# Layer one's sum holds h+1: an ELU from one Exp and one two-operand pass, and seven of eight steps of the second layer in split precision

## The chip, the core and the metric

One core of one Trainium2 chip. The metric is the device time of one launch in microseconds (us), median of three runs. Engines: TensorE (PE) multiplies matrices; VectorE (DVE), ScalarE (ACT) and GpSimd (POOL) work elementwise; SyncE (SP) issues the transfers. Matmuls write PSUM, everything else lies in SBUF.

## The reference

Agent attention and a two-layer network on its output. There are two batches of 12480 tokens of 128 channels, 49 agents, and a hidden width of 2048. Nothing but fp32 goes in and comes out, except for the weights, which are fp64.

```python
a2k = softmax(scale * agents @ k.T)          # per batch, 49 x 12480
agent_v = a2k @ v                            # 49 x 128
q2a = softmax(scale * q @ agents.T)          # 12480 x 49
x = (q2a @ agent_v).reshape(24960, 128)
h = x @ w_in                                 # 24960 x 2048
g = np.where(h > 0, h, np.exp(np.minimum(h, 0)) - 1)
out = g @ w_out                              # 24960 x 128
```

## The kernel before

**Layers.** `agent_v @ w_in` is folded into one matrix A of 49 rows and 2048 columns per batch, so the first layer is `h = q2a @ A`. The tokens come in 26 groups of 960 (13 per batch); a group has two halves of 480 columns. A half is worked through in eight steps (`NP`), each with 256 rows of the hidden width as two tiles of 128. That makes S = 416 steps. In a step:

- `p1` (matmul at L413) makes `h` of both tiles in two PSUM banks. Probabilities `p` and matrix A are both split into a high part in fp32r (fp32 cut to fewer bits) and a low part, the remainder. Products are high x high, high x low and low x high; the two tiles lie on rows 0 to 48 and 64 to 112 of the operands, so their matmuls run in pairs side by side.
- `elu` makes g: ACT computes `e = Relu(-h)` (L419) and `e = Exp(-e)` (L422) in place, DVE computes `g = max(e - 1, h)` (L424), reading `h` from PSUM.
- `split`, in the steps whose number modulo 8 is in `SPLITS`, makes `hi = fp32r(g)` on DVE (L431) and, in two passes on POOL, `lo0` and `lo1`, each `g - hi` of one tile (by the helper `rest`, L204). In the last step of all, those two run on DVE.
- `p2` (L453), four steps later (`LAG = 4`; three at the very start), adds the second layer of a step into two PSUM banks. A plain step multiplies g and `w_f` in fp32: four matmuls, which the profile shows as eight records. A split step has twelve in fp32r: hi x w_lo, hi x w_hi, lo x w_hi. Rows 0 to 63 and 64 to 127 go to different banks, again as pairs side by side.
- After the last of eight steps, the two banks are added: DVE copies one (`ob`, L465), ACT the other (`oa`, L468, called `rest_of_sum` and placed between Relu and Exp of the step), POOL adds them (L469) and SP stores.

**Order.** The order of each engine's queue is written out by hand: the main loop at the end (from L719) issues per step `p1`, `p2` of four steps before, the work listed in `mid`, `elu`, `split`, then the work listed in `pre` by `at(s, ...)`. Engines run their queues in order. `h` has three slots in PSUM, shared with the attention's work; tile `e` has 2 buffers, `g` 5, `hi` 3, `lo0` and `lo1` 3 each.

**Attention among the steps.** The scores and maxima of the groups of q, and for the second batch those of k and the sum with v, are done in visits (`plan`, `visit`): in some steps, one slot of PSUM takes the scores of two groups (L291, L160), and DVE and ACT turn them into probabilities over the next steps (maxima L296, L303, Exp L307, sums L311, `pp` L325, transposes L331, parts `px` and `py` L345 to L350). In the late half there is one visit with two q groups in every 32 steps.

**Prologue.** Before the loop the first batch's attention is done, and the fp64 weights are turned into fp32 by integer steps (`f64_steps`, whose ACT passes are L103 and L105), `w_out` also into `w_f`, or `w_hi` (ACT, L199) and `w_lo` (POOL, L204). At the end stand the sum with v (L219), its transposition (L238, L239) and A for the first batch (L257, `A_hi`, `A_lo`). At s = 2 there is one matmul (L731) whose result nobody reads.

```python
    SPLITS = ((1, 3, 4, 6, 7), (1, 4, 6, 7))

    def is_split(s):
        j, half, c = at_step(s)
        return c in SPLITS[half if j * NM + NP + LAG in covered else 0]
```

So a half has five or four split steps; in the late part of the kernel 19 of 32.

Of the kernel before, what the change touches and what calls it, by code (L numbers as in the profile page):

```python
# [24 lines left out]
def tile_agent_attention_moe(  # L25
# [14 lines left out]
    NA2 = ROWS[1] + NA  # L40
# [23 lines left out]
    wc_p = ctx.enter_context(tc.tile_pool(name="wc", bufs=2))  # L64
# [272 lines left out]
    def q_parts(j, part):  # L337
# [10 lines left out]
        a, b = [slice(r, r + NA) for r in ROWS]  # L348
# [15 lines left out]
    def wo_step(c):  # L364

        if c not in wo_gen:
            parts = []
            for i in range(2):
# [4 lines left out]
                else:  # L373
                    w_e[x] = wc_p.tile([128, 256], F32, tag="even", name="even")
# [41 lines left out]
    def elu(s, between=None):  # L416

        h, e = h_t.pop(s), x_p.tile([128, 2, T], F32, tag="e", name="e")
        nc.scalar.activation(out=e, in_=h, func=ACTF.Relu, scale=-1.0)  # L419
        if between:  # L420
            between()
        nc.scalar.activation(out=e, in_=e, func=ACTF.Exp, scale=-1.0)  # L422
        g = g_p.tile([128, 2, T], F32, tag="g", name="g", bufs=5)
        nc.vector.scalar_tensor_tensor(out=g, in0=e, scalar=-1.0, in1=h, op0=ALU.add, op1=ALU.max)  # L424
        g_t[s] = g

    def split(s):
        if not is_split(s):
            return
        hi_t[s] = g_p.tile([128, 2, T], F32R, tag="hi", name="hi", bufs=3)  # L430
        nc.vector.tensor_copy(out=hi_t[s], in_=g_t[s])  # L431
        lo_t[s] = []
        for i in range(2):
            lo_t[s].append(g_p.tile([128, T], F32R, tag=f"lo{i}", name=f"lo{i}", bufs=3))
            rest(nc.vector if s == S - 1 else nc.gpsimd, lo_t[s][i], g_t[s][:, i, :], hi_t[s][:, i, :])

    def p2(s):
# [16 lines left out]
        if last:  # L454
# [325 lines left out]
```

## Time and profile before

| | |
|---|---|
| median of three runs | 998.79 us (998.23 to 1000.27) |
| profiled execution, first to last instruction | 995.9 us |
| PE, DVE, ACT, POOL busy | 978.3, 849.7, 884.3, 687.0 us |
| mean granted clock of PE | 0.996 |

The profile is of one execution, for which the page gives the span from first to last instruction and no other time; the runs' times have 2.9 us around it at the median. Times inside are us from the start of the span; an engine's busy time is the union of its instructions. Matmuls overlap in the pipeline, so the mean duration of one is no price; the chain's pieces are.

### The profile page before, as it was taken

The page shows a single profiled execution, that of the slowest core. Times are in us where ns is not written, and L with a number is a line of the kernel's source. Part 1 is how long each engine was busy: PE and PEld are TensorE (multiplying, and loading weights), DVE is VectorE, ACT ScalarE, POOL GpSimd, SP SyncE. Part 2 cuts the span into 40 slices and gives each one's busy share as a digit, 9 for nine tenths or more (in the row PEclk, how much of TensorE's full clock was granted, in tenths as well). Part 3 has the DMA queues.
Part 4 walks back from the last instruction along what each step waited for, and adds up shares of the span by engine and source line. Part 5 has one row for each costly group of instructions (what it writes and reads, how often), then busy time and mean ns, then how long its engine had stood idle before and what let it go on. Part 6 is the DMA issues. An engine that isn't in the chain of part 4 may idle for free.

```text
span 995.9 us, 25483 instructions
## 1 busy us (share of the span) xinstructions
PE 978.3 (98%) x10380; PEld 734.3 (74%) x10380; DVE 849.7 (85%) x1028; ACT 884.3 (89%) x1017; POOL 687.0 (69%) x559
## 2 busy tenths in 40 slices
PE   7899999999999999999999999999999999999998
PEld 5767777777777777877777777777777777777775
DVE  7778888888888878888888898898888888988887
ACT  4588998988988889998998999989999989989996
POOL 3146666666666766766786886877868867867886
PEclk8999999999999999999999999999999999999999
DMA  9942222223232211101101101011020021001000
GB/s 349 385 148 89 80 72 81 78 74 96 68 85 66 66 41 46 38 31 65 36 23 55 37 26 62 26 56 41 18 76 27 21 66 37 26 12 37 27 20 21
DMA packets 25983, 67.30 MB, mean 68 GB/s; under 512 B 3083, under 2 KB 14963, under 8 KB 25867
## 3 DMA queue, kind: packets, MB, share of 16 engines
q1 hardware_dynamic: 25867, 65.69, 19.5%
q8 instruction: 81, 1.33, 0.6%
q14 instruction: 35, 0.29, 0.1%
HBM read 43.11 MB, written 12.78 MB: 56 GB/s over the span
## 4 chain that ended last, share of the span: by engine, by line
PE 93%; DVE 2%; ACT 2%; DMA 2%; issue 1%; POOL 0%; SPq 0%; DVEq 0%; ACTq 0%
PE o L453 59%; PE h L413 27%; PE h L291 2%; PE h L219 2%; PE h L160 1%; DMA v<-in_vx_dram 1%; PE h L331 1%; DVE g L424 1%; DMA k<-in_kT_dram 1%; ACT e L419 1%; ACT e L422 0%; PE o L160 0%; DVE m_all L168 0%; DVE ex L107 0%; ACT ex L103 0%
## 5 line engine op out<-in xcount | busy, mean ns | idle before, releaser
L204 POOL TENSOR_TENSOR lo<-g,hi 128x480 fp32r<-128x480 f32 x484 | 603.3, 1272 | 253.6 <-DVE hi L431 190.3
L424 DVE SCALAR_TENSOR_TENSOR g<-e,h 128x960 f32<-128x960 f32 x416 | 478.2, 1150 | 109.2 <-ACT e L422 91.7
L419 ACT ACTIVATE e<-h 128x960 f32<-128x960 f32 x416 | 402.5, 967 | 41.0 <-PE h L413 38.5
L422 ACT ACTIVATE e<-e 128x960 f32<-128x960 f32 x416 | 419.1, 1007 | 11.6
L453 PE MATMUL o<-g,w_f 64*128 64x480 f32 x1384 | 307.8, 562 | 0.2 <-DVE g L424 0.2
L413 PE MATMUL h<-py,ahi 49*128 49x480 f32 x832 | 292.4, 431 | 1.4 <-DVE g L424 0.7
L413 PE MATMUL h<-px,ahi 49*128 49x480 f32 x832 | 292.4, 431 | 0.1
L431 DVE CAST hi<-g 128x960 fp32r<-128x960 f32 x243 | 198.4, 816 | 10.8
L453 PEld LDWEIGHTS o<-g,w_f 64*128 64x128 f32 x1384 | 133.2, 185 | 83.1 <-issue 73.6
L413 PEld LDWEIGHTS h<-py,ahi 49*128 49x128 f32 x832 | 149.9, 186 | 39.3 <-issue 23.4
L413 PEld LDWEIGHTS h<-px,ahi 49*128 49x128 f32 x832 | 149.9, 186 | 26.3 <-issue 17.0
L453 PE MATMUL o<-hi,w_lo 64*128 64x480 f32 x972 | 159.4, 403 | 0.0
L413 PE MATMUL h<-px,alo 49*128 49x480 f32 x416 | 157.0, 377 | 0.0
L413 PE MATMUL h<-py,alo 49*128 49x480 f32 x416 | 157.0, 377 | 0.0
L453 PE MATMUL o<-lo,w_hi 64*128 64x480 f32 x972 | 146.9, 378 | 0.0
L453 PE MATMUL o<-hi,w_hi 64*128 64x480 f32 x972 | 146.0, 376 | 0.0
L453 PEld LDWEIGHTS o<-hi,w_lo 64*128 64x128 f32 x972 | 93.4, 186 | 26.0 <-issue 14.3
L453 PEld LDWEIGHTS o<-lo,w_hi 64*128 64x128 f32 x972 | 92.6, 184 | 13.6 <-POOL lo L204 0.3
L453 PEld LDWEIGHTS o<-hi,w_hi 64*128 64x128 f32 x972 | 92.5, 184 | 13.0
L413 PEld LDWEIGHTS h<-py,alo 49*128 49x128 f32 x416 | 76.6, 184 | 5.7
L413 PEld LDWEIGHTS h<-px,alo 49*128 49x128 f32 x416 | 76.6, 184 | 5.6 <-DVE alo L275 0.2
L469 POOL TENSOR_TENSOR ob<-ob,oa 128x480 f32<-128x480 f32 x51 | 70.0, 1372 | 12.2 <-ACT oa L468 12.2
(89 smaller groups left out, 517.7 us busy)
## 6 DMA issues: line engine op xcount, KB each, us to landing
k<-in_kT_dram SPq DMA_DIRECT2D x26, 480.0 KB
q<-in_qT_dram SPq DMA_DIRECT2D x26, 480.0 KB
out_dram<-ob SPq DMA_DIRECT2D x51, 240.0 KB
py<-px SPq DMA_DIRECT2D x104, 91.9 KB
v<-in_vx_dram SPq DMA_DIRECT2D x13, 516.0 KB
v<-in_vx_dram SPq DMA_DIRECT2D x13, 483.8 KB
raw<-in_w_in_dram SPq DMA_DIRECT2D x4, 512.0 KB
raw<-in_w_out_dram SPq DMA_DIRECT2D x4, 512.0 KB
```

The costliest lines, as they stand in the source:

```text
L160: nc.tensor.matmul(out=ps[u:u + w, j * NA:(j + 1) * NA], lhsT=src[:, x:x + w], rhs=ag_sb[:, b, :], start=True, stop=True)
L204: eng.tensor_tensor(out=out, in0=x, in1=hi.bitcast(F32), op=ALU.subtract)
L219: nc.tensor.matmul(out=ps[u:u + 64], lhsT=e[:, j * NA:j * NA + 64], rhs=v_t[b, r][:, j, :], start=(r == rs[0] and j < 2), stop=(r == rs[-1 ...
L291: nc.tensor.matmul(out=ps[u:u + w, t * NA:(t + 1) * NA], lhsT=src[:, x:x + w], rhs=ag_sb[:, j // NG, :], start=True, stop=True)
L331: nc.tensor.transpose(ps[:NA2, u, i * HP:(i + 1) * HP], pp[x, i, 0:NA2], ident[x, x])
L413: nc.tensor.matmul(out=h[:, u, 0:T], lhsT=a[x, :], rhs=p[u ^ half][x, :], start=i == 0, stop=i == 2)
L419: nc.scalar.activation(out=e, in_=h, func=ACTF.Relu, scale=-1.0)
L422: nc.scalar.activation(out=e, in_=e, func=ACTF.Exp, scale=-1.0)
L424: nc.vector.scalar_tensor_tensor(out=g, in0=e, scalar=-1.0, in1=h, op0=ALU.add, op1=ALU.max)
L431: nc.vector.tensor_copy(out=hi_t[s], in_=g_t[s])
L453: nc.tensor.matmul(out=o_t[u][:, 0:T], lhsT=w[x], rhs=v[x, :], start=first and i == 0, stop=last and i == len(jobs) - 1)
L469: nc.gpsimd.tensor_tensor(out=ob, in0=ob, in1=oa, op=ALU.add)
```

## The change

**Sum.** Both rows of probabilities get a 50th row of ones (`NK = NA + 1`; written once into `pp`), and A's high part gets a 50th row of ones, by a bias tile `unit` that is 1 in that row and 0 elsewhere (`A_hi`). So PSUM holds h+1. ELU+1 is then `max(min(exp(h), 1), h + 1)`: ACT's single pass is `Exp(x - 1)`, with a bias tile `mone`, and DVE's pass takes minimum and maximum in one. The Relu is gone.

**Constant.** As g is too large by 1, the output is too large by the column sums of `w_out`. `w_sums` has PE add these up from the weights' parts with matmuls of two columns, 22 in the prologue and 8 at s = 2 (in place of L731's), DVE negates them into `ncs`, and `oa` adds them as a bias.

**Split.** `PLAIN = (3,)`: one step in eight is plain. The cast to `hi` goes from DVE to ACT. Of the lo passes, `lo1` goes to DVE in steps 0, 2 and 7 of eight. `hi` has 4 buffers.

**Order.** `split` of a step is issued in the next step, after that one's `elu` and `rest_of_sum`. The pool of the conversions (`wc`) ends with the prologue.

```diff
-    SPLITS = ((1, 3, 4, 6, 7), (1, 4, 6, 7))
-    SPLIT = tuple(c for c in range(NP) if c in SPLITS[0] or c in SPLITS[1])
-    PLAIN = tuple(c for c in range(NP) if c not in SPLITS[0] or c not in SPLITS[1])
+    PLAIN = (3,)
+    SPLIT = tuple(c for c in range(NP) if c not in PLAIN)
+    LO_DVE = (0, 2, 7)
...
-            nc.scalar.activation(out=h, in_=A_ps(b, lo, hi), func=ACTF.Copy, scale=av["rz"][:, 0:1])
+            nc.scalar.activation(out=h, in_=A_ps(b, lo, hi), func=ACTF.Identity, scale=av["rz"][:, 0:1], bias=unit[:NA2, 0:1])
...
-                x = slice(r, r + NA)
+                x = slice(r, r + (NK if i == 0 else NA))
                 nc.tensor.matmul(out=h[:, u, 0:T], lhsT=a[x, :], rhs=p[u ^ half][x, :], start=i == 0, stop=i == 2)
...
-    def elu(s, between=None):
+    def elu(s):
 
         h, e = h_t.pop(s), x_p.tile([128, 2, T], F32, tag="e", name="e")
-        nc.scalar.activation(out=e, in_=h, func=ACTF.Relu, scale=-1.0)
-        if between:
-            between()
-        nc.scalar.activation(out=e, in_=e, func=ACTF.Exp, scale=-1.0)
+        nc.scalar.activation(out=e, in_=h, func=ACTF.Exp, bias=mone, scale=1.0)
         g = g_p.tile([128, 2, T], F32, tag="g", name="g", bufs=5)
-        nc.vector.scalar_tensor_tensor(out=g, in0=e, scalar=-1.0, in1=h, op0=ALU.add, op1=ALU.max)
+        nc.vector.scalar_tensor_tensor(out=g, in0=e, scalar=1.0, in1=h, op0=ALU.min, op1=ALU.max)
         g_t[s] = g
 
     def split(s):
-        if not is_split(s):
+        if not 0 <= s < S or not is_split(s):
             return
-        hi_t[s] = g_p.tile([128, 2, T], F32R, tag="hi", name="hi", bufs=3)
-        nc.vector.tensor_copy(out=hi_t[s], in_=g_t[s])
+        hi_t[s] = g_p.tile([128, 2, T], F32R, tag="hi", name="hi", bufs=4)
+        cast_hi(nc.scalar, hi_t[s], g_t[s])
         lo_t[s] = []
         for i in range(2):
+            eng = nc.vector if s == S - 1 or i and s % NP in LO_DVE else nc.gpsimd
             lo_t[s].append(g_p.tile([128, T], F32R, tag=f"lo{i}", name=f"lo{i}", bufs=3))
-            rest(nc.vector if s == S - 1 else nc.gpsimd, lo_t[s][i], g_t[s][:, i, :], hi_t[s][:, i, :])
+            rest(eng, lo_t[s][i], g_t[s][:, i, :], hi_t[s][:, i, :])
...
-                nc.scalar.activation(out=oa, in_=pa[:, 0:T], func=ACTF.Copy)
+                nc.scalar.activation(out=oa, in_=pa[:, 0:T], func=ACTF.Identity, bias=ncs[:, 0:1])
...
+    def w_sums(ps, xs):
+        jobs = []
+        for x in xs:
+            for i in range(2):
+                if x in PLAIN:
+                    jobs.append((w_f[:, PLAIN.index(x), i], one2))
+                if x in SPLIT:
+                    jobs += [(w[:, SPLIT.index(x), i], one2r) for w in (w_hi, w_lo)]
+        for n, (w, o) in enumerate(jobs):
+            nc.tensor.matmul(out=ps, lhsT=w, rhs=o, start=n == 0, stop=n == len(jobs) - 1)
...
+            for r in ROWS:
+                dve.memset(pp[:, :, r + NA:r + NK], 1.0)
+            dve.memset(mone, -1.0)
...
             loads("q1 K0 K1")
+            w_sums(hk[:, 1, 0:2], range(6))
+            dve.tensor_scalar(out=ncs, in0=hk[:, 1, 0:2], scalar1=-1.0, scalar2=None, op0=ALU.mult)
             for r in range(6, NR):
...
-                nc.tensor.matmul(out=t[:, 0:T], lhsT=ident, rhs=win_sb[:, 0:T], start=True, stop=True)
+                w_sums(t[:, 0:2], range(6, NP))
+                dve.tensor_tensor(out=ncs, in0=ncs, in1=t[:, 0:2], op=ALU.subtract)
...
             if s < S:
-                elu(s, after)
-                split(s)
-            elif after:
+                elu(s)
+            if after:
                 after()
+            split(s - 1)
```

ACT's queue in the late half, around one copy of the output: Relu and Exp of each step before (`e` from `h`, then `e` in place).

```order
L419 ACTIVATE e_8535<-h_8516 128x960
L422 ACTIVATE e_8535<-e_8535 128x960
L419 ACTIVATE e_8563<-h_8540 128x960
L468 ACTIVATE oa_8559<-o0_8375 128x480
L422 ACTIVATE e_8563<-e_8563 128x960
L419 ACTIVATE e_8597<-h_8577 128x960
```

The same place after the change:

```order
L424 ACTIVATE e_9056<-h_9037,mone_92 128x960
L205 ACTIVATE hi_9060<-g_9029 128x960
L424 ACTIVATE e_9088<-h_9066,mone_92 128x960
L471 ACTIVATE oa_9085<-o0_8870,ncs_96 128x480
L205 ACTIVATE hi_9095<-g_9058 128x960
L424 ACTIVATE e_9195<-h_9174,mone_92 128x960
```

Each Exp is followed by the cast of the step before; the output copy stands behind the step's Exp and ahead of that cast.

DVE's queue around the `pp` pass before (the ELU pass `g`, then its cast `hi` in the split steps):

```order
L465 COPY ob_7621<-o1_7437 128x480
L325 TENSOR_TENSOR pp_86<-qe_7423,z_7507 124x2x4x49
L424 SCALAR_TENSOR_TENSOR g_7630<-e_7624,h_7601 128x960
L431 CAST hi_7632<-g_7630 128x960
L424 SCALAR_TENSOR_TENSOR g_7661<-e_7658,h_7638 128x960
L431 CAST hi_7663<-g_7661 128x960
```

And after, there and two to three steps on:

```order
L468 COPY ob_7807<-o1_7605 128x480
L331 TENSOR_TENSOR pp_83<-qe_7093,z_7677 124x2x4x49
L426 SCALAR_TENSOR_TENSOR g_7812<-e_7810,h_7787 128x960
L210 TENSOR_TENSOR lo1_7821<-g_7779,hi_7817 128x480
L426 SCALAR_TENSOR_TENSOR g_7853<-e_7851,h_7823 128x960
```

The casts are gone, and a `lo1` pass stands behind the ELU pass of the next step.

POOL's queue, one half of a group after the change (step 4 of eight first):

```order
L210 TENSOR_TENSOR lo0_8906<-g_8886,hi_8904 128x480
L210 TENSOR_TENSOR lo1_8908<-g_8886,hi_8904 128x480
L210 TENSOR_TENSOR lo0_8935<-g_8902,hi_8933 128x480
L210 TENSOR_TENSOR lo1_8937<-g_8902,hi_8933 128x480
L210 TENSOR_TENSOR lo0_8975<-g_8931,hi_8973 128x480
L210 TENSOR_TENSOR lo1_8977<-g_8931,hi_8973 128x480
L210 TENSOR_TENSOR lo0_9004<-g_8971,hi_9002 128x480
L210 TENSOR_TENSOR lo0_9033<-g_9000,hi_9031 128x480
```

Steps 7 and 0 have their `lo0` alone on POOL; step 1's two, an `ob` and step 2's `lo0` follow, 11 lo passes and one `ob` in eight steps, where a half had 8 or 10 and one `ob` before.

## Rows read from the trace of the kernel before

**Rows 1.** The page, busy time of each engine over the span.

```profile
PE 978.3 (98%) x10380; PEld 734.3 (74%) x10380; DVE 849.7 (85%) x1028; ACT 884.3 (89%) x1017; POOL 687.0 (69%) x559
```

**Rows 2.** The page, chain of work that ended last, by line.

```profile
PE o L453 59%; PE h L413 27%; PE h L291 2%; PE h L219 2%; PE h L160 1%; DMA v<-in_vx_dram 1%; PE h L331 1%; DVE g L424 1%; DMA k<-in_kT_dram 1%; ACT e L419 1%; ACT e L422 0%; PE o L160 0%; DVE m_all L168 0%; DVE ex L107 0%; ACT ex L103 0%
```

**Rows 3.** Stretches: length; busy PE, PEld, DVE, ACT, POOL; granted clock, DMA share, GB/s.

```profile
0.00:57.50 57.50, 46.11 (x737) 37.18 (x737) 40.74 (x89) 29.41 (x55) 15.50 (x24) 0.94 0.94 360
57.50:991.70 934.20, 932.18 (x9645) 697.16 (x9643) 808.27 (x938) 854.24 (x961) 671.46 (x535) 1.00 0.16 50
755.75:825.00 69.25, 69.25 (x672) 52.34 (x670) 61.01 (x70) 64.87 (x73) 52.92 (x43) 1.00 0.12 41
```

**Rows 4.** Chain in order of time, 755.75 to 825: start, us, what.

```profile
759.33 0.65 PE h L413 x6
759.98 1.61 PE o L453 x8
...
762.65 1.30 PE o L453 x12
```

**Rows 5.** Groups by line: busy us, mean ns | idle before, releasers.

```profile
L204 POOL TENSOR_TENSOR lo<-g,hi 128x480 fp32r<-128x480 f32 x484 | 603.3, 1272 | 253.6 <-DVE hi L431 190.3 <-PE h L413 32.2 <-DVE z L319 25.8
L424 DVE SCALAR_TENSOR_TENSOR g<-e,h 128x960 f32<-128x960 f32 x416 | 478.2, 1150 | 109.2 <-ACT e L422 91.7 <-POOL lo L204 6.0 <-PE h L413 3.8
L422 ACT ACTIVATE e<-e 128x960 f32<-128x960 f32 x416 | 419.1, 1007 | 11.6
L419 ACT ACTIVATE e<-h 128x960 f32<-128x960 f32 x416 | 402.5, 967 | 41.0 <-PE h L413 38.5 <-DVE g L424 1.0 <-DVE z L316 0.7
L453 PE MATMUL o<-g,w_f 64*128 64x480 f32 x1384 | 307.8, 562 | 0.2 <-DVE g L424 0.2
...
L431 DVE CAST hi<-g 128x960 fp32r<-128x960 f32 x243 | 198.4, 816 | 10.8
...
L103 ACT ACTIVATE ex<-ex,ebias 128x512 int32<-128x512 int32 x8 | 5.8, 722 | 6.5 <-DVE ex L99 6.5
...
L105 ACT ACTIVATE fr<-fr 128x512 f32<-128x512 int32 x8 | 5.0, 622 | 0.7 <-DVE fr L101 0.7
```

**Rows 6.** Timeline, end of the prologue: start, us, engine, what [idle before].

```profile
44.47 5.74 PE L219 MATMUL h<-v,s_all 120*64 120x129 f32 x96
...
51.86 0.47 PE L238 MATMUL h<-dup,sv 128*128 128x113 f32 x2 [0.39 <-DVE sv L227]
...
52.17 0.27 PE L239 MATMUL h<-sv,dup 128*113 128x1 f32 x2
...
57.56 1.07 PE L731 MATMUL o<-win_sb,ident 128*128 128x480 f32 x2
...
58.87 1.84 PE L453 MATMUL o<-g,w_f 64*128 64x480 f32 x7 [0.23 <-DVE g L424]
```

**Rows 7.** Timeline around one pp pass of DVE.

```profile
437.38 2.43 POOL L204 TENSOR_TENSOR lo<-g,hi 128x480 fp32r<-128x480 f32 x2 [1.07 <-DVE hi L431]
...
439.42 0.82 DVE L325 TENSOR_TENSOR pp<-qe,z 124x392 f32<-124x392 f32 x1
...
439.76 1.55 POOL L469 TENSOR_TENSOR ob<-ob,oa 128x480 f32<-128x480 f32 x1
```

**Rows 8.** Tile lo: count, duration in ns least/median/most, first and last start.

```profile
L204 POOL TENSOR_TENSOR lo<-g,hi x484: 1200/1227/1653, 61.1 to 988.2; 128x480 fp32r<-128x480 f32 x162
L204 DVE TENSOR_TENSOR lo<-g,hi x2: 645/1070/1495, 988.9 to 990.3; 128x480 fp32r<-128x480 f32 x2
```

**Rows 9.** Timeline: one split step from Relu to its lo matmuls.

```profile
599.64 0.97 ACT L419 ACTIVATE e<-h 128x960 f32<-128x960 f32 x1 [0.92 <-PE h L413]
...
604.06 2.39 POOL L204 TENSOR_TENSOR lo<-g,hi 128x480 fp32r<-128x480 f32 x2 [4.46 <-DVE hi L431]
...
609.09 0.60 PE L453 MATMUL o<-lo,w_hi 64*128 64x480 f32 x4
```

**Rows 10.** Timeline of DVE: first of the four passes of a visit.

```profile
808.42 0.56 DVE L296 TENSOR_REDUCE mx<-h 124x8 f32<-124x392 f32 x1
```

More of the change, by code (lines that the diff above doesn't have):

```diff
@@ L39, in tile_agent_attention_moe @@
     ROWS = (0, 64)
-    NA2 = ROWS[1] + NA
+    NK = NA + 1
+    NA2 = ROWS[1] + NK
     DFF = w_in.shape[1]
@@ L63, in tile_agent_attention_moe @@
     sm_p = ctx.enter_context(tc.tile_pool(name="sm", bufs=2))
-    wc_p = ctx.enter_context(tc.tile_pool(name="wc", bufs=2))
+    conv_pool = []
     ps_o = ctx.enter_context(tc.tile_pool(name="ps_o", bufs=1, space=bass.MemoryType.PSUM))
@@ L81, in tile_agent_attention_moe @@
     ebias = const.tile([128, 1], F32)
+    mone = const.tile([128, 1], F32)
+    unit = const.tile([128, 1], F32)
+    one2 = const.tile([128, 2], F32)
+    one2r = const.tile([128, 2], F32R)
+    ncs = const.tile([128, 2], F32)
     def f64_load(src, pool=None):
@@ L85, in f64_load @@
         if pool is None:
-            raw = wc_p.tile([128, n, 2], I32, tag="raw", name="raw", bufs=4)
+            raw = conv_pool[0].tile([128, n, 2], I32, tag="raw", name="raw", bufs=4)
         else:
@@ L95, in f64_steps @@
         low, top = raw[:, :, 0].bitcast(U32), raw[:, :, 1]
-        fr = wc_p.tile([128, n], I32, tag="fr", name="fr")
-        ex = wc_p.tile([128, n], I32, tag="ex", name="ex")
+        fr = conv_pool[0].tile([128, n], I32, tag="fr", name="fr")
+        ex = conv_pool[0].tile([128, n], I32, tag="ex", name="ex")
         m = fr.bitcast(F32)
@@ L254, in A_pe @@
         w = win_sb[:, lo:hi].rearrange("p (m i f) -> p m i f", i=2, f=128)
-        for i, (r, n) in enumerate(zip(ROWS, (64, NA))):
+        for i, (r, n) in enumerate(zip(ROWS, (64, NK))):
             out = av[b, lo][r:r + n, 0:(hi - lo) // 2].rearrange("p (m f) -> p m f", f=128)
@@ L264, in A_hi @@
         if eng is nc.vector:
-            nc.vector.tensor_scalar(out=h, in0=A_ps(b, lo, hi), scalar1=av["rz"][:, 0:1], scalar2=None, op0=ALU.mult)
+            nc.vector.tensor_scalar(out=h, in0=A_ps(b, lo, hi), scalar1=av["rz"][:, 0:1], scalar2=unit[:NA2, 0:1], op0=ALU.mult, op1=ALU.add)
         else:
-            nc.scalar.activation(out=h, in_=A_ps(b, lo, hi), func=ACTF.Copy, scale=av["rz"][:, 0:1])
+            nc.scalar.activation(out=h, in_=A_ps(b, lo, hi), func=ACTF.Identity, scale=av["rz"][:, 0:1], bias=unit[:NA2, 0:1])
         l = a_p.tile([NA2, 2, 128], F32R, tag="alo", name="alo")
@@ L347, in q_parts @@
             rest(nc.vector, by_half(x), q_st[j].pop("tr"), by_half(p_t[j][0][0]))
-        a, b = [slice(r, r + NA) for r in ROWS]
+        a, b = [slice(r, r + (NA if part else NK)) for r in ROWS]
         nc.sync.dma_start(out=y[a].bitcast(F32), in_=x[b].bitcast(F32))
@@ L373, in wo_step @@
                 else:
-                    w_e[x] = wc_p.tile([128, 256], F32, tag="even", name="even")
+                    w_e[x] = conv_pool[0].tile([128, 256], F32, tag="even", name="even")
                 parts.append((w_e[x], y))
@@ L401, in is_split @@
     def is_split(s):
-        j, half, c = at_step(s)
-        return c in SPLITS[half if j * NM + NP + LAG in covered else 0]
+        return at_step(s)[2] in SPLIT
     def p1(s):
@@ L460, in p2 @@
                 for x in (slice(0, T // 2), slice(T // 2, T)):
-                    nc.scalar.activation(out=oa[:, x], in_=pa[:, x], func=ACTF.Copy)
+                    nc.scalar.activation(out=oa[:, x], in_=pa[:, x], func=ACTF.Identity, bias=ncs[:, 0:1])
                     nc.vector.tensor_tensor(out=ob[:, x], in0=pb[:, x], in1=oa[:, x], op=ALU.add)
@@ L481, in tile_agent_attention_moe @@
     with tc.manual_schedule():
-        with tc.tile_pool(name="pro", bufs=6) as pro:
+        with tc.tile_pool(name="pro", bufs=6) as pro, tc.tile_pool(name="wc", bufs=2) as wc_p:
+            conv_pool.append(wc_p)
             win_r, win_gen = {}, {}
@@ L529, in tile_agent_attention_moe @@
             dve.memset(pp, 0.0)
+            for r in ROWS:
+                dve.memset(pp[:, :, r + NA:r + NK], 1.0)
+            dve.memset(mone, -1.0)
+            dve.memset(one2, 1.0)
+            dve.tensor_copy(out=one2r, in_=one2)
+            dve.tensor_tensor(out=unit, in0=ident[:, ROWS[0] + NA:ROWS[0] + NK], in1=ident[:, ROWS[1] + NA:ROWS[1] + NK], op=ALU.add)
             for r in ROWS:
```

## The prediction

> **What bounds the kernel now.** I read the page first: over the span of 995.9 us TensorE (PE) is busy 98%, ScalarE (ACT) 89%, VectorE (DVE) 85%, GpSimd (POOL) 69% [rows 1]. Busy shares alone don't name the bound, so I went to the chain of work that ended last: PE in the second layer's line is 59% of the span, PE in the first's 27% [rows 2]. Cut by stage, PE has 932.18 us of the 934.20 us from 57.5 us on, the loop of 416 steps, and its granted clock is 1.00 there, the level of 2.4 GHz [rows 3]. So in the loop nobody makes PE wait: a step costs what its matmuls cost, and the other three engines fit underneath. The chain in order of time gives the price of each piece [rows 4]: a first layer (6 matmuls) 0.65 us, a second layer that is **split** (12) 1.30 us, one that is **plain** (8 records) 1.61 us. The plain group counts 1384 records, that is 173 steps, and the casts of g, one in each split step, 243 [rows 5]. The profiled span of 995.9 us is 2.9 us below the median time of 998.79 us; I sum on the span and add 2.9.
>
> **The change, part by part.**
>
> *PE, second layer.* One of eight steps stays plain: 416/8 = 52, and 121 plain steps become split. 121 x (1.61 - 1.30) = **-37.5 us**, all on the path, since PE is the path [rows 2 to 4]. The first layer's high weights grow from 49 to 50 rows with the same 480 columns: nothing.
>
> By the Trainium skill's page "VectorE: DVE Perf Modes", the section on the TRN2 errata, a matmul costs 6 plus its columns in cycles, so 486/2.4 GHz = 0.2025 us (an estimate from that page). Six pairs would take 1.22 us, a converted step would give 0.40 and not 0.31, and the sum would be some 11 us lower. The 1.30 us of the row decides here.
>
> *PE, sums of the weights.* The prologue gets 22 narrow matmuls (24 records), where PE is on the path. No row shows matmuls of two columns. The 129-column ones beside them take 5.74/96 = 0.06 us a record, those of one column 0.27/2 = 0.135, which are nearest in shape, those of 113 with 128 rows of weights 0.47/2 = 0.235 [rows 6]. 24 x 0.135 = **+3.2 us**, bounds 1.4 (0.06) and 5.6 (0.235). The eight at s = 2 take 1.1 and replace a piece of 1.07 [rows 6]: nothing. Two more w_hi and w_lo passes and a few DVE fills of one to four columns lie in the prologue, where in 57.5 us ACT is busy 29.4, DVE 40.7 and POOL 15.5 [rows 3]: nothing.
>
> *Start of the loop.* Step 0 was plain and is split. Its second layer began at 58.87 us, right behind the ELU pass g [rows 6]; now a cast of 1.0 us stands between: **+1.0 us**, bounds 0 and 2.5 (if the lo passes are waited for too).
>
> *ACT.* A step had Relu and Exp, 0.967 + 1.007. Now it has one Exp from PSUM with a bias tile and, in 7 of 8 steps, a cast. A pass with a bias tile takes 722 ns where one of the same size without takes 622, so I price Exp at 0.967 + 0.10 and the cast like the Exp from SBUF, 1.007 [rows 5]. 416 x 1.067 + 364 x 1.007 + 51 x 0.10 for the output copies = 815 us against 821: 6 us less busy time, up to 53 less if the bias costs nothing. ACT has 854.2 in the loop [rows 3], so 801 to 848 of some 900: 89 to 94%. Cover remains, but less than it seems: the cast of step s stands between Exp of s+1 and Exp of s+2 and waits for DVE, for which ACT's Relu hardly waited (1.0 us in all) [rows 5].
>
> *DVE.* It loses 243 casts, 198.4 us [rows 5], and gains 155 lo passes (157 where there were 2). They read two SBUF tensors, as the pp pass does. Such a pass stands while POOL's pass runs, and POOL's next one is lengthened: pp starts at 439.42, POOL's lo ends at 439.81, pp ends 0.43 later, and POOL's next pass takes 1.55 us [rows 7] where 1.20 is its least [rows 8]. A lo pass on DVE costs 0.645 alone and up to 1.495, as the two at the end of this trace [rows 8]. DVE in the loop: 808.3 - 198.4 + 155 x (0.645 to 1.495) = 710 to 842 us, 79 to 94% of 900. It isn't the bound even at the dear end.
>
> *POOL.* It goes from 484 lo passes to 571. Alone, two in a row take 2.39 us [rows 9], 1.195 each; with today's casts in their way the mean is 1.272 [rows 5]. In 32 late steps it has 44 lo and 4 ob passes from now on, and 14 DVE passes that hold it up, 0.35 for the 392 columns of pp, so some 0.43 for 480: 48 x 1.195 + 14 x 0.43 = 63.4 us, dear end 48 x 1.272 + 14 x 0.43 = 67.1. PE needs 69.25 us for 32 such steps now [rows 3], 19 split and 13 plain; with 28 and 4 it needs 69.25 - 9 x 0.31 = 66.5. POOL has 95 to 101% of that. This is the tightest place, and nothing covers it.
>
> *Lead.* A step's second layer follows four steps behind its first. Today: ACT takes up a first layer at 599.64, both lo are done at 606.45, 6.8 us later, and lo is read at 609.09 [rows 9]. After the change the lead from the end of a first layer is 1.30 + 3 x (0.65 + 1.30) + 0.65 = 7.80 us, and two thirds of 1.30 until lo is read: 8.67. The chain: the ELU pass ends near 0.1 + 1.07 + 0.1 + 1.15 = 2.4, but the cast stands behind the next step's Exp, which ends at 1.95 + 0.1 + 1.07 = 3.1; cast 1.01, hand-off 0.2, two POOL passes 2.4: 6.7 us (durations from [rows 5, 9], hand-offs estimated from the gaps there). Margin 1.9. At a visit with two q groups DVE runs four passes of 0.56 ahead of the next ELU pass [rows 10], 2.3 us, 0.4 past the margin; with a like one for each of 13 pairs of groups that is **+5 us**, bounds 0 and the rivals below.
>
> *End.* Of the last four steps one plain one becomes split (counted above); the way to the last lo has one ACT pass and one DVE cast less and one ACT cast more: nothing, within 1 us.
>
> Sum: 995.9 - 37.5 + 3.2 + 1.0 + 5 = 967.6, plus 2.9: 970.5 us. I say **970**, 2.9% faster.
>
> **The rivals.**
>
> A. *POOL becomes the bound.* For it: 95 to 101% of PE's time, and its idle time today, 190.3 us of it for hi [rows 5], is of a kind that can't be saved up, as three lo buffers let it run only three steps ahead. Against: it has a free step in every eight, and no DVE cast stands in its way any more. At the dear end 67.1 against 66.5 costs 0.6, and one hole of up to a microsecond in 32 steps as much again; over 13 such stretches 8 to 21 us: 978 to 991, say **984 us**. The Trainium skill's "SBUF — State Buffer", section "Who interferes with whom", speaks against the change here: a DVE pass with two SBUF inputs and a GpSimd pass that reads SBUF exclude each other for the whole instruction. By that rule, the trace agrees.
>
> B. *The four-step lead isn't enough.* Place: the second layer's lo matmuls, waiting for POOL. One whole pair of lo passes ahead in POOL's queue (2.4 + 0.43) makes the chain 9.6 us against 8.67; 0.93 over 4.4 steps is 0.21 us a step, 416 x 0.21 = 87 us on top of 965: about **1050 us**. It decides from 8.67 on, and the whole gain of 28 us (0.067 a step, 0.3 of lead) is gone at 9.0. For it: a shorter lead than today's 9.4, and a cast that waits for two engines. Against: the margin of 1.9, and that PE idles only 2.0 us in the whole loop now [rows 3].
>
> C. *Split steps run at the plain pace.* 1.61/8 = 0.201 a pass, six passes 1.21: 0.40 x 121 = 48 us, **959 us**. The page on VectorE above has nearly that figure. Against: the chain shows 1.30 for a split piece [rows 4].
>
> D. *The gain is eaten in small pieces.* The ring of one ELU pass, its cast, the next Exp but one and its ELU pass takes 1.15 + 1.01 + 1.07 and hand-offs, 3.5 us for two steps, and 3.9 where a lo pass of 1.495 stands in place of Exp's 1.07, against PE's 3.9. It bounds nothing alone, but makes up lost time slowly. With a wait of 0.06 us a step, 25 us in all: **996 us**. That the change doesn't do what it says is out: its rows above show one Exp a step, the casts on ACT and the lo passes on two engines.
>
> **How the numbers follow.** Forecast (961 to 977) 0.56; A 0.26; B 0.10; C 0.03; D 0.05. The likeliest case gives 970. Its cheap end is 995.9 - 37.5 + 1.4 + 2.9 = 963, and 961 without the 2.0 us that PE idles in the loop today; C takes the range to 959, A to 990. B and D lie outside. A measurement of this kernel tells about 0.2%, 2 us, from no change. Faster: the forecast, A, C and a part of D, 0.86; same 0.04; slower 0.10.
>
> **What will show it.** Right: in the chain split pieces of 1.30, a plain one of 1.61 in every eight, first layers of 0.65; PE over 99% busy from its first step to the last; 32 late steps in 66 to 67 us; Exp near 1.07 and hi casts near 1.01 on ACT; POOL over 90% busy in the loop, with passes of 1.55 to 1.65 where DVE's lo passes cross it. A: PE gaps that end with POOL's lo, and POOL at 97% or more. B: such gaps at nearly every split step, with POOL idle between. D: PE gaps that end with DVE's g. Wrong altogether: split pieces that aren't 1.30, a granted clock below 1.00 in the loop, or a prologue that ends over 6 us later.

## The result and the profile after

The changed kernel takes 971.50 us at the median of four runs (970.83 to 973.33), the kernel before 998.51 in the same session (997.61 to 1000.27). The ratio is 0.9734, with a 95% interval of 0.972 to 0.9748: 27.0 us or 2.7% faster. 970 was predicted, 959 to 990 the range. The execution that was profiled is the slowest of the four, 973.33 us with a span of 971.6.

The page after, busy time by engine and the chain of work that ended last, by engine and by line [rows 1, 2]:

```profile
PE 949.6 (98%) x10894; PEld 796.2 (82%) x10894; DVE 807.5 (83%) x948; ACT 847.6 (87%) x967; POOL 833.8 (86%) x648
...
PE 79%; DVE 11%; issue 4%; ACT 3%; POOL 1%; DMA 1%; SPq 0%; POOLq 0%; DVEq 0%; ACTq 0%
```

TensorE is 98% busy as before and loses 28.7 us of work; GpSimd gains 147. The chain has changed: before, TensorE's lines held over nine tenths of it; now TensorE holds 79%, DVE, ACT and POOL together 15%. TensorE is still the bound, but it is met by the others at some places. Where, the stretches of the loop tell [rows 3] (the second and third are 32 late steps each, from the second layer of step 314 to that of 346 and on to that of 378):

```profile
57.50:967.00 909.50, 902.53 (x10167) 756.07 (x10163) 766.21 (x856) 819.75 (x913) 816.40 (x622) 1.00 0.17 51
757.84:824.98 67.14, 66.96 (x706) 55.98 (x704) 57.84 (x63) 62.08 (x69) 62.72 (x48) 1.00 0.13 42
824.98:892.14 67.16, 66.93 (x706) 57.15 (x704) 57.92 (x63) 62.09 (x69) 62.73 (x48) 1.00 0.08 27
```

32 late steps take 67.15 us where they took 69.25. POOL is busy 62.7 of them, 93%. The groups by line, shapes apart [rows 5, 8], show the new passes at the prices that were reckoned, Exp with a bias tile 1061 ns, the cast 1003, and a lo pass on POOL 1339:

```profile
L210 POOL TENSOR_TENSOR lo<-g,hi 128x480 fp32r<-128x480 f32 x571 | 744.3, 1339 | 96.6 <-ACT hi L205 37.4 <-issue 35.8 <-PE o L456 23.1
...
L424 ACT ACTIVATE e<-h,mone 128x960 f32<-128x960 f32 x416 | 440.9, 1061 | 40.9 <-PE h L418 31.7 <-DVE g L426 6.3 <-ACT hi L205 0.3
L205 ACT ACTIVATE hi<-g 128x960 fp32r<-128x960 f32 x364 | 365.0, 1003 | 23.2 <-DVE g L426 22.7
...
L210 DVE TENSOR_TENSOR lo<-g,hi 128x480 fp32r<-128x480 f32 x157 | 165.2, 1053 | 1.1 <-ACT hi L205 1.1
```

The chain in order of time over the first of the two stretches [rows 4]:

```profile
758.00 1.30 PE o L456 x12
759.30 0.66 PE h L418 x6
759.96 1.61 PE o L456 x8
...
774.04 1.46 PE o L456 x12
...
789.13 0.49 DVE mx L302
```

A split second layer costs 1.30, a plain one 1.61, as before. Some split pieces are longer: 1.46 at 774.04, the third of eight steps (step 322). And where the visit with two q groups stands, the chain leaves TensorE and runs through DVE's four passes. The timeline has what follows from that visit:

```profile
789.06 0.55 DVE L302 TENSOR_REDUCE mx<-h 124x8 f32<-124x392 f32 x1
...
791.20 2.21 DVE L426 SCALAR_TENSOR_TENSOR g<-e,h 128x960 f32<-128x960 f32 x2
...
793.52 13.06 POOL L210 TENSOR_TENSOR lo<-g,hi 128x480 fp32r<-128x480 f32 x10 [3.29 <-PE o L456]
806.54 1.67 POOL L472 TENSOR_TENSOR ob<-ob,oa 128x480 f32<-128x480 f32 x1
808.17 4.76 POOL L210 TENSOR_TENSOR lo<-g,hi 128x480 fp32r<-128x480 f32 x4
...
809.46 0.70 PE L456 MATMUL o<-lo,w_hi 64*128 64x480 f32 x4 [0.18 <-POOL lo L210]
```

While DVE serves the visit, no new g comes, and POOL stands idle for 3.29 us. (The row names TensorE's L456 as what ended the wait; the cast that POOL waits for, behind that g, ended only 0.06 us earlier, at 793.39.) Then POOL has ten lo passes without a hole, 13.06 us, and the sum of an output; the lo pass of step 338, seven steps behind the visit's, begins at 808.17 and is there at 809.46, when TensorE has wanted it for a moment already. The profile books only 0.18 us as idle there, but the piece of that step, from its first matmul's start to its last one's end, takes 1.94 us where its neighbours take 1.46 to 1.50, and TensorE's next piece starts 0.48 us late.

At the start the trace shows the sums of the weights and, behind them, a slower clock [rows 6] (TensorE's timeline; then the granted clock, last but two of the columns, in three stretches of 4 us):

```profile
45.15 0.27 PE L488 MATMUL h<-one2r,w_hi 128*128 128x2 f32 x1
...
48.06 7.87 PE L225 MATMUL h<-v,s_all 120*64 120x129 f32 x112
...
58.59 0.48 PE L418 MATMUL h<-px,ahi 50*128 50x480 f32 x1 [0.24 <-ACT ahi L273]
...
64.42 0.49 PE L456 MATMUL o<-hi,w_lo 64*128 64x480 f32 x1 [1.34 <-ACT hi L205]
```

```profile
44.00:48.00 4.00, 4.00 (x48) 3.76 (x44) 2.71 (x6) 2.94 (x7) 0.00 (x0) 0.96 0.91 362
48.00:52.00 4.00, 4.00 (x45) 3.98 (x47) 1.36 (x3) 1.60 (x4) 2.28 (x4) 0.61 0.59 159
64.00:68.00 4.00, 3.31 (x15) 2.59 (x17) 2.28 (x4) 2.22 (x3) 3.40 (x3) 0.60 0.00 0
```

And the end, where POOL's six lo passes of steps 412 to 414 run behind TensorE (timeline):

```profile
957.96 7.51 POOL L210 TENSOR_TENSOR lo<-g,hi 128x480 fp32r<-128x480 f32 x6 [1.14 <-issue]
...
960.71 1.16 DVE L426 SCALAR_TENSOR_TENSOR g<-e,h 128x960 f32<-128x960 f32 x1 [0.67 <-ACT e L424]
...
963.00 2.99 DVE L210 TENSOR_TENSOR lo<-g,hi 128x480 fp32r<-128x480 f32 x2 [1.13 <-ACT hi L205]
...
965.52 0.49 PE L456 MATMUL o<-lo,w_hi 64*128 64x480 f32 x2 [1.08 <-POOL lo L210]
```

### The profile page after: what moved, and what is told of

The parts are those of the page before. It is cut to its first block, busy times and chain, and to the rows that moved or that the text cites. A ratio compares the mean times of both kernels' runs of the same rounds, so it can differ in the third digit from the quotient of the medians.

```text
span 971.6 us, 26490 instructions
## 1 busy us (share of the span) xinstructions
PE 949.6 (98%) x10894; PEld 796.2 (82%) x10894; DVE 807.5 (83%) x948; ACT 847.6 (87%) x967; POOL 833.8 (86%) x648
## 4 chain that ended last, share of the span: by engine, by line
PE 79%; DVE 11%; issue 4%; ACT 3%; POOL 1%; DMA 1%; SPq 0%; POOLq 0%; DVEq 0%; ACTq 0%
PE o L456 49%; PE h L418 24%; DVE g L426 4%; PE h L225 3%; DVE lo L210 2%; ACT e L424 2%; POOL lo L210 1%; PE h L297 1%; PE h L166 1%; DVE ob L468 1%; DVE pp L331 1%; ACT hi L205 1%; DVE m_all L174 1%; DMA k<-in_kT_dram 1%; DVE mx L302 1%
## 5 line engine op out<-in xcount | busy, mean ns | idle before, releaser
L210 POOL TENSOR_TENSOR lo<-g,hi 128x480 fp32r<-128x480 f32 x571 | 744.3, 1339 | 96.6 <-ACT hi L205 37.4
L424 ACT ACTIVATE e<-h,mone 128x960 f32<-128x960 f32 x416 | 440.9, 1061 | 40.9 <-PE h L418 31.7
L205 ACT ACTIVATE hi<-g 128x960 fp32r<-128x960 f32 x364 | 365.0, 1003 | 23.2 <-DVE g L426 22.7
L418 PE MATMUL h<-py,ahi 50*128 50x480 f32 x832 | 273.3, 408 | 1.1 <-DVE m_all L174 1.0
L418 PE MATMUL h<-px,ahi 50*128 50x480 f32 x832 | 273.7, 408 | 0.6 <-DVE g L426 0.4
L456 PE MATMUL o<-lo,w_hi 64*128 64x480 f32 x1456 | 224.5, 380 | 3.6 <-POOL lo L210 3.6
L456 PE MATMUL o<-hi,w_lo 64*128 64x480 f32 x1456 | 222.3, 378 | 1.6 <-ACT hi L205 1.3
L456 PE MATMUL o<-hi,w_hi 64*128 64x480 f32 x1456 | 221.3, 376 | 0.0
L418 PEld LDWEIGHTS h<-py,ahi 50*128 50x128 f32 x832 | 149.8, 186 | 22.4 <-issue 9.4
L418 PEld LDWEIGHTS h<-px,ahi 50*128 50x128 f32 x832 | 149.9, 186 | 20.9 <-issue 11.6
L210 DVE TENSOR_TENSOR lo<-g,hi 128x480 fp32r<-128x480 f32 x157 | 165.2, 1053 | 1.1 <-ACT hi L205 1.1
L456 PEld LDWEIGHTS o<-lo,w_hi 64*128 64x128 f32 x1456 | 141.5, 184 | 25.8 <-POOL lo L210 9.8
L456 PEld LDWEIGHTS o<-hi,w_lo 64*128 64x128 f32 x1456 | 143.9, 186 | 19.3 <-ACT hi L205 1.6
L456 PEld LDWEIGHTS o<-hi,w_hi 64*128 64x128 f32 x1456 | 142.8, 184 | 16.2
L456 PE MATMUL o<-g,w_f 64*128 64x480 f32 x416 | 92.6, 562 | 0.0
L456 PEld LDWEIGHTS o<-g,w_f 64*128 64x128 f32 x416 | 40.6, 185 | 24.1 <-issue 21.6
```

What stands on the lines that cost most here:

```text
L205: nc.scalar.activation(out=out, in_=x, func=ACTF.Copy)
L210: eng.tensor_tensor(out=out, in0=x, in1=hi.bitcast(F32), op=ALU.subtract)
L418: nc.tensor.matmul(out=h[:, u, 0:T], lhsT=a[x, :], rhs=p[u ^ half][x, :], start=i == 0, stop=i == 2)
L424: nc.scalar.activation(out=e, in_=h, func=ACTF.Exp, bias=mone, scale=1.0)
L456: nc.tensor.matmul(out=o_t[u][:, 0:T], lhsT=w[x], rhs=v[x, :], start=first and i == 0, stop=last and i == len(jobs) - 1)
```

## The experiments

The theory: 121 cheaper second layers pay 37.5 us; the sums, the start and small waits for lo take some 10 back. The rivals said that the gain is elsewhere, or that POOL, the lead or the clock takes more.

### Which part pays

**The new ELU with the old split steps.**

```diff
-    PLAIN = (3,)
+    SPLITS = ((1, 3, 4, 6, 7), (1, 4, 6, 7))
...
```

> The change with the split pattern of before (243 split steps, 173 plain), everything else kept: one Exp a step, h+1, casts on ACT, lo1 of step 7 on DVE. Theory (the gain is the second layer's pieces on PE, 0.31 us for each of 121 steps): 971.5 + 37.5 - some 4 us of lo waits that vanish = 1004 us (1001 to 1008), slower than the kernel before by the start's cost; PE over 99% in the loop. Rival (the shorter ELU, a pass less on ACT and a cast less on DVE, gives a share of its own): under 997 us.

Measured 999.54 us, ratio 1.0016 (1.0007 to 1.0025): under the theory's 1001 to 1008 and over the rival's 997. On balance the whole gain is in the converted steps. But the rival is right in part, for the shorter ELU has a share of its own in the loop: from the first ELU pass to that of step 400, this kernel is 5.6 us quicker than the one before (6.2 us late at step 0, 0.5 at step 400). What the change adds ahead of the loop eats that.

**The old ELU with the new split steps** (seven of eight split, lo passes shared as in the change, casts on DVE).

```diff
-    SPLITS = ((1, 3, 4, 6, 7), (1, 4, 6, 7))
+    SPLITS = ((0, 1, 2, 4, 5, 6, 7), (0, 1, 2, 4, 5, 6, 7))
+    LO_DVE = (0, 2, 7)
...
```

> The kernel before with only the new split pattern and lo1 of steps 0, 2, 7 on DVE: Relu and Exp on ACT, casts on DVE as before. Theory (the new ELU and the moved casts are the cover that the split needs): DVE would need 808 + 121 x 0.82 + 155 x 1.05 = 1070 us for the loop against PE's 900, so DVE bounds it: 1130 us (1080 to 1180), DVE 97% or more in the loop, PE waiting for g and hi. Rival (PE's pieces alone decide, the cover wasn't needed): 962 to 975 us.

Measured 1242.4 us in one run, further out than the 1080 to 1180 that were expected. Its page, busy time and chain:

```profile
PE 1065.4 (86%) x10864; PEld 886.1 (71%) x10864; DVE 1113.8 (90%) x1304; ACT 892.9 (72%) x1019; POOL 878.6 (71%) x648
...
DVE 43%; PE 39%; issue 9%; ACT 5%; POOL 2%; DMA 1%; DVEq 1%; SPq 0%; POOLq 0%; ACTq 0%
```

DVE is the bound, as the theory has it, but it is 90% busy and not 97: its work was counted right and taken for gapless. While TensorE waits, its granted clock is lower besides (0.93 in the mean), which the expectation didn't have. So the split steps pay only with work taken off DVE. That it must be the casts, and that ACT had no room for them beside the Relu, was reckoned and not run.

### Where the limit of split steps lies

**All eight steps split.**

```diff
-    PLAIN = (3,)
+    PLAIN = ()
...
```

> No plain step at all: 416 split steps, lo1 of steps 0, 2, 7 on DVE. PE's own work falls by 52 x 0.31 = 16 us. Theory (POOL's free step in eight is what lets it keep up): 13 x 1.2 + 1.2 + 3 x 0.43 + 0.2 = 18.3 us for eight steps on POOL against 16.5 on PE, 52 x 18.3 + 72 = 1024 us (1000 to 1035), POOL 98% in the loop. Rival (PE stays the bound): 956 us.

Measured 1031.2 us in one run, as the theory has it. Page, then the weight loads that wait for lo:

```profile
PE 967.6 (94%) x11102; PEld 797.5 (77%) x11102; DVE 818.1 (79%) x948; ACT 884.3 (86%) x1020; POOL 955.0 (93%) x753
```

```profile
L456 PEld LDWEIGHTS o<-lo,w_hi 64*128 64x128 f32 x1664 | 159.6, 185 | 101.0 <-POOL lo L210 76.9 <-DVE lo L210 4.7
```

52 more steps at 0.31 would save 16 us; TensorE's weight loads wait 77 for POOL instead, which is 98% busy from its first lo pass to its last. The one plain step in eight is POOL's time to catch up, and it is needed.

**All lo passes on POOL.**

```diff
-    LO_DVE = (0, 2, 7)
+    LO_DVE = ()
```

> All lo passes on POOL, none on DVE (but for the last step). Theory (POOL is at its edge; its passes at 1.2 us a piece set the pace beyond it): 14 x 1.2 + 1.2 + 0.2 = 18.2 us for eight steps against PE's 16.8, 52 x 18.2 + 64 before POOL's first + 8 after its last = 1018 us (1005 to 1030), POOL 98% or more of the loop, DVE down by 165 us. Rival (POOL has room, DVE's lo passes are what disturbs): 972 us or less.

Measured 1083.5 us in one run: the direction is right, the size is not. From its first lo pass at 65.7 us to the end of its last at 1075.3 POOL is 92% busy and not 98. Its lo passes got shorter, 1244 ns in place of 1339, now that no lo pass of DVE crosses them, but there is idle time before them:

```profile
L210 POOL TENSOR_TENSOR lo<-g,hi 128x480 fp32r<-128x480 f32 x726 | 870.7, 1244 | 91.3 <-PE h L418 45.1 <-PE o L456 22.3 <-ACT hi L205 17.8
```

Of the 91.3 us, 11.3 lie ahead of the first lo pass of the loop; 80 are holes in the loop, where POOL has 929.6 us of work. The expectation counted POOL's work and took it for gapless. The releasers in the row, most of them TensorE's pieces, fit a ring: a late POOL stops TensorE, a late TensorE stops ACT and DVE, and these then feed POOL late. So an engine that sets the pace isn't busy all the time here.

**Four and five of eight second lo passes on DVE**, in place of three.

```diff
-    LO_DVE = (0, 2, 7)
+    LO_DVE = (0, 2, 5, 7)
```

> lo1 of step 5 goes to DVE too: 4 of 14 lo passes of eight steps on DVE, 10 on POOL. Theory (what the loop loses against PE's own time are waits for POOL's lo): POOL falls from 90 to some 84% of the loop, DVE rises from 84 to some 90%, PE's weight loads wait less for POOL, time 968 us (966 to 971). Rival (DVE's lo passes delay the ELU pass, and with it cast and Exp): 974 us or more, with PE waits that end with DVE's g or ACT's hi.

Measured 968.80 us (968.54 to 969.04), 2.7 below the changed kernel. Its chain, 32 late steps from step 314 to 346 and the next 32, and lo on both engines:

```profile
PE 94%; DVE 3%; ACT 1%; DMA 1%; issue 0%; POOL 0%; SPq 0%; POOLq 0%; DVEq 0%
```

```profile
755.35:821.88 66.53, 66.53 (x707) 58.35 (x705) 58.42 (x67) 61.24 (x69) 59.53 (x45) 1.00 0.13 42
821.88:888.38 66.50, 66.50 (x707) 56.19 (x704) 58.59 (x67) 61.30 (x69) 59.57 (x45) 1.00 0.09 28
```

```profile
L210 POOL TENSOR_TENSOR lo<-g,hi 128x480 fp32r<-128x480 f32 x519 | 699.5, 1375 | 136.4 <-ACT hi L205 65.0 <-issue 39.0 <-PE o L456 23.1
...
L210 DVE TENSOR_TENSOR lo<-g,hi 128x480 fp32r<-128x480 f32 x209 | 193.7, 927 | 1.5 <-ACT hi L205 1.3
```

This is the plainest experiment of all. TensorE fills the 32 steps without a gap, in the 66.5 us that its pieces cost. So the 0.63 us that the changed kernel has more are waits that go when POOL is relieved. With the three steps 4 to 6 wholly on POOL, that engine had six passes in a row, some 7.5 us against 5.9 of TensorE's, and had little room left behind a visit; moving one of the six was enough. No run moves the pass of another step instead, so that it is this row of six that counts, and not POOL's mean load alone, isn't shown. With five:

> The changed kernel with the second lo of five steps in eight on VectorE (0, 2, 4, 5, 7) in place of three. Theory (VectorE's side is now the one near its limit: each further step adds about 52 passes of 0.9 us, so it would be busy over 88% of the span, and the waits come back as waits for g and the two-bank visits): 970 (968.5 to 975). Rival (GpSimd alone sets the waits of the loop, and each step taken off it helps): under 968.

Measured 978.16 us, ratio 0.9799 (0.9785 to 0.9812): slower than with three, and beyond the 975 that the theory allowed. Page and chain:

```profile
PE 949.1 (97%) x10894; PEld 796.6 (82%) x10894; DVE 902.4 (93%) x1052; ACT 838.8 (86%) x967; POOL 721.2 (74%) x544
...
PE 62%; DVE 19%; issue 9%; ACT 8%; DMA 2%; POOL 0%; DVEq 0%; SPq 0%; ACTq 0%
```

DVE at 93% is past its limit, POOL at 74% has room to spare. Of three, four and five, four is the best.

### The cast's place

**The cast of a step right behind its own Exp**, not behind the next one's.

```diff
                 elu(s)
+                split(s)
             if after:
                 after()
-            split(s - 1)
```

> The cast of a step is issued right behind its own Exp and not behind the next step's. Theory (ACT's queue is in order, so the cast then holds ACT until DVE's ELU pass of the same step is done): 1.06 + 1.15 + 1.0 + 0.2 of hand-offs = 3.4 us for a split step, 364 x 3.4 + 52 x 2.0 + 64 = 1400 us (1250 to 1450), ACT idle some 500 us before hi, ended by DVE's g. Rival (the place of the cast in the queue doesn't matter as long as four steps of lead are there): 970 to 980 us.

Measured 1413.7 us in one run, as the theory has it. ACT's casts by line:

```profile
L205 ACT ACTIVATE hi<-g 128x960 fp32r<-128x960 f32 x364 | 366.7, 1008 | 518.8 <-DVE g L426 509.4 <-PE o L456 5.4 <-PE h L418 4.1
```

509 us of waiting for DVE, 1.4 a cast: the full latency of the ELU pass, with the next Exp queued behind it. The order that the change chose costs 23 us of such waits in all. (A mean clock of 0.90 adds to this run too.)

### The start

**No sums.** This kernel leaves out the subtraction of the weights' column sums.

```diff
-            w_sums(hk[:, 1, 0:2], range(6))
-            dve.tensor_scalar(out=ncs, in0=hk[:, 1, 0:2], scalar1=-1.0, scalar2=None, op0=ALU.mult)
+            dve.memset(ncs, 0.0)
...
```

> The change without the column sums of the weights: 22 narrow matmuls in the prologue and 8 at s = 2 are left out (the old matmul that nobody reads is back at s = 2), so the output is too large by the column sums of w_out. Theory (the narrow matmuls cost 2.9 us themselves and bring the granted clock down to 0.6 for some 4 us twice): clock 1.00 from 40 to 70 us, first step's first layer back near 54 us, time 966 us (964.5 to 967.5). Rival (they cost their own time only): 968.6 us, with the clock still low somewhere between 44 and 70 us.

Measured 968.19 us (967.74 to 969.11): the sums cost 3.3 us at the median, so the time is nearer the rival's 968.6 than the theory's 966. The clock is as the theory had it: 1.00 from 44 to 80 us in this run's profile, without the two dips of the changed kernel.

**The same sums with 128 columns.**

```diff
-    one2 = const.tile([128, 2], F32)
+    one2 = const.tile([128, 128], F32)
...
```

> The sums with 128 equal columns of ones in place of 2, same count of matmuls and same result. Theory (the clock fell because the array had hardly any columns to stream): granted clock 1.00 from 44 to 56 us, the stretch of the sums no longer than now (2.9 us), first layer of step 0 about 1.5 us earlier, time 969 us (967 to 970.5). Rival (the clock falls for the waits around it, not for the narrow matmuls): clock 0.6 in 48 to 52 as now, time 971 to 974.

Measured 971.40 us (970.58 to 971.8), the same as the changed kernel; the theory missed, and the time is the rival's. The profiled execution, the fastest of the five, did have a granted clock of 1.00 from 40 to 60 us, and the 112 pieces of attention behind the sums took 6.39 us in place of 7.87, but over the runs nothing is left of it. Whether the narrow pieces bring the lower clock isn't settled either: of seven profiled executions with them at 45 us (the changed kernel, and the runs with the old split steps, with zero, four and five steps on DVE, with all steps split and with the early cast), six took 7.9 to 9.2 us for those 112 pieces, one 6.40.

**Early sums**: 14 of the 22 in the place of a filler where TensorE waits for the maximum's chain, the rest at s = 2.

```diff
             k_max_last()
-            busy(1, 256)
+            w_sums(two[:, 1, 256:258], range(4))
...
-            w_sums(hk[:, 1, 0:2], range(6))
-            dve.tensor_scalar(out=ncs, in0=hk[:, 1, 0:2], scalar1=-1.0, scalar2=None, op0=ALU.mult)
+            dve.tensor_scalar(out=ncs, in0=two[:, 1, 256:258], scalar1=-1.0, scalar2=None, op0=ALU.mult)
...
```

> The changed kernel, with 14 of the column sums' matmuls (steps 0 to 3) put where TensorE waits for the maximum's chain before the loop (2.24 us idle and 0.70 us of filler there in the changed kernel's trace), and only the others in the loop. Theory: the sums cost the 2.9 us that they take on TensorE's path, and those that fill a wait are free: some 1.8 us less than the changed kernel's 971.5, so 969.7 (968.5 to 970.7). Rival (the cost is the clock after the sums, which 2-column pieces bring wherever they stand): 971 or above.

Measured 975.60 us (975.19 to 977.12), slower. The number lies where the rival had it, but for another cause. DVE's and TensorE's timelines show why:

```profile
48.95 0.68 DVE L115 SCALAR_TENSOR_TENSOR fr<-raw,fr 128x512 f32<-128x512 uint32 x1
49.55 0.15 DVE L624 TENSOR_SCALAR ncs<-h 128x2 f32<-128x2 f32 x1
```

```profile
49.81 8.90 PE L225 MATMUL h<-v,s_all 120*64 120x129 f32 x112 [4.33 <-ACT fr L111]
```

The sums now share a PSUM tile with the attention's accumulator. TensorE's next product waits until DVE has read the sums, and I had left that pass behind the conversion of the last weights in DVE's queue. (The row names ACT's L111, but that was done at 48.83; DVE's pass ends at 49.70, and where it stands earlier, in the last run below, the wait is gone.) 4.33 us of idle TensorE, and then a granted clock of 0.52 to 0.63 for 8 us. The same mistake is in the next run, which adds the four steps on DVE and moves the second lo of the last step but one to DVE too:

> The early sums and four steps of eight with their second lo on VectorE together, and the last step but one's second lo on VectorE too. Theory: the three gains add, 971.5 - 2.7 - 1.8 - 0.5 = 966.5 (965 to 968). Rival (the gains overlap, since a TensorE that starts earlier only waits longer for lo): 968 to 969.

Measured 970.76 us (969.59 to 971.02). Its first layer starts at 62.04, 2.6 us later than in the run with four steps on DVE; so this one didn't test its theory. The mended kernel has DVE's pass behind `k_max_b` (all three edits, and this):

```diff
             k_max_b(hk[:, 1, :])
+            dve.tensor_scalar(out=ncs, in0=two[:, 1, 256:258], scalar1=-1.0, scalar2=None, op0=ALU.mult)
```

> As the run with early sums and four steps of eight on VectorE, but with VectorE's pass that reads the early sums right behind the maximum's chain, and no longer behind the conversion of the last weights, for whose end (49.6 us) TensorE's second stretch of attention products waited 4.3 to 5.6 us. Theory (that wait alone hid the gain): first layer some 5 us earlier than in that run's 62.04, and 966.5 (965 to 968) in all. Rival (early sums bring nothing, the clock after the stretch of small pieces sets the start): 968.8 or above.

Measured **963.14 us** (962.42 to 963.23), ratio 0.965 (0.9637 to 0.9663): 8.4 us below the changed kernel, and under the 965 to 968 that adding up the gains had given. TensorE's timeline:

```profile
45.07 6.39 PE L225 MATMUL h<-v,s_all 120*64 120x129 f32 x112
...
54.12 0.48 PE L418 MATMUL h<-px,ahi 50*128 50x480 f32 x1 [0.24 <-ACT ahi L273]
```

The first layer starts at 54.12, where the kernel before had it at 54.11; in the run with four steps on DVE it was 59.48. Those 5.4 us are the sums' 2.8, the 1.7 that the same 112 pieces took longer (8.06 us there, 6.39 here), and 0.9 in the stretch ahead of the sums. From the last ELU pass's start to TensorE's end it takes 5.3 us instead of 6.6.

## Why the prediction was right, step by step

- **Converted steps, -37.5 us.** Right. Pieces of 1.30 and 1.61, as said. Where nothing waits, in the run with four steps on DVE, 32 late steps take 66.5 us, the very figure that the prediction had for TensorE alone; before it was 69.25 [rows 3]. By the Trainium skill's "VectorE: DVE Perf Modes" (the section on the TRN2 errata) split pieces would have been 1.22, an estimate from its 6 plus 480 cycles; the trace disagrees with that, 1.30 here too.
- **Sums, +3.2.** Right in the median, 971.50 - 968.19 = 3.3. In the profiled execution they cost more: 22 matmuls took 2.9 us (0.12 a record instead of 0.135), the pieces behind them ran up to 1.5 us longer at a granted clock of 0.61, and the first layer starts at 58.59, 4.5 us later than before. The prediction had no term for a lower clock, and named it only for the loop.
- **Start of the loop, +1.0.** Right: TensorE waited 1.34 us for the first cast and 0.27 for the sums' pass on DVE, within the bounds of 0 to 2.5. Not foreseen was the clock of 0.60 from 64 to 68 us: the first split piece takes 2.2 us from 65.18 on, though a split piece costs 1.30. The run without sums waits 1.32 for the same cast, at a clock of 1.00.
- **Waits in the loop, +5.** Right in size, partly by luck. 32 late steps lose 0.63 us (67.15 less 66.52), and 6.5 such stretches make 4.1. The cause that was named is there: a visit with two q groups stops DVE, the lead's margin is gone, and 0.48 of the 0.63 is lost behind it. But there are seven such visits, where the prediction put 0.4 on each of 13 pairs. The other 0.15 is lost at step 322, with no such visit close ahead. The early half, from the ELU pass of step 8 to that of step 208, loses some 2 us more, most of them in the run with four steps on DVE too; their cause stays open. What the prediction had wrong is the place in the program where TensorE feels a visit: not at the first step behind it but at the third of an eight, seven steps later, since POOL has a long unbroken row of lo passes by then. Nor had it a gain for the shorter ELU. Against the run with the old split steps, which is 5.6 us quicker in the loop than the kernel before, the converted steps lose 12.4 us of their 37.5 in the loop; the two partly cancel.
- **End, 0 within 1.** Wrong, by a little: from the last ELU pass to TensorE's end it is 6.6 us, 4.9 before. POOL still has six lo passes of the steps before the last when the last ones come, and DVE's two passes, 0.645 and 1.495 before [rows 8], take 2.99 together as POOL's passes cross them. The step of the prediction that failed looked at the way of the last step alone and left out what stands in POOL's queue ahead of it.
- **The sum.** -37.5 + 3.3 + 1.6 + 4.1 + 1.7 = -26.8; measured -27.0. That they agree so closely is luck. The 3.3 is from medians, the rest from the profiled execution, the slowest of its four, whose span is only 24.4 us shorter than before (971.6 against 995.9). There, -37.5 goes with 4.5 up to the first layer, 6.8 from the first ELU pass to the last, and 1.7 at the end.
- **POOL, rival A.** 63.4 us of work in 32 late steps was reckoned and 62.7 measured, 93% of TensorE's 67.15, not the 97% that was the sign for A. With one more converted step in eight A comes true (POOL 98% busy in the loop); with all lo on POOL the time goes up and TensorE waits for lo, but POOL has 92%.
- **Lead, rival B.** TensorE waits in 32 late steps come to 0.63 us, so the margin held at most steps. No run shortens the lead alone: the run with the early cast is slower by more than 400 us because ACT's queue waits, and its price isn't B's.
- **The signs.** TensorE is busy 99.2% from 57.5 us on (902.53 of 909.50), and 32 late steps take 67.15 us, just over the 66 to 67; POOL has 89.8% there, a hair under the 90 that were named, with passes of 1.64 to 1.67 where DVE's cross them. One sign of being wrong altogether did show for a moment: the clock of 0.60 from 64 to 68 us lies in the loop, whose mean is still 1.00.
- **The shared port.** The Trainium skill's "SBUF — State Buffer", section "Who interferes with whom", says that DVE passes with two SBUF inputs and GpSimd passes that read SBUF lock each other out. The trace agrees, and puts a price on it: POOL's mean lo pass is 1244 ns with no lo on DVE, 1339 with three in eight steps, 1375 with four.

## What to carry to other kernels

When an engine near its limit feeds the bound one, count its passes by position and not only on the mean: here three steps in a row that all lean on it come just where TensorE's waits are, while the mean still shows 7% free. And a small piece of work that is moved into a wait must be followed to its reader: the reader's place in its own queue decides whether the move pays.

## What the runs showed of the hardware that was not expected

- The granted clock of TensorE falls to some 0.6 in the mean of 4 us, so mostly to the level of 1.2 GHz, after a stretch of two-column matmuls or of idling in the prologue (0.61 from 48 to 52 us in the changed kernel, 0.52 from 48 to 52 us, with 4.33 us of idling up to 49.81, in the run with early sums), and not in every execution of like stretches. In the loop's start it is 0.60 from 64 to 68 us in the changed kernel, behind eight two-column matmuls and 1.34 us of idling; the run without sums idles 1.32 us there and keeps 1.00. What decides it wasn't found.
- Two-column matmuls with 128 rows and columns of weights follow each other by 0.11 us, as those of 128 columns do: both sets of sums took 2.8 to 2.9 us.
- TensorE's waits for lo hide inside its busy time: 0.18 us is booked as idle where a step's piece costs 0.48 more, and over 32 steps 0.18 of 0.63. The length of pieces is the better measure.
